# End of a fused attention and FFN kernel: PSUM banks, order of feature sums, and the engine of one elementwise pass

## The chip, the cores and the metric

The kernel runs on one core of one Trainium2 chip. The metric is device time in microseconds (us) for one execution, as the median of several. The engines are TensorE (PE, matmuls; its weight loads are shown as PEld), VectorE (DVE), ScalarE (ACT), GpSimd (POOL) and SyncE (SP, which issues the DMAs here). All engines run their own instruction streams and wait for each other by semaphores.

## The reference

Batch B = 8, H = 8 heads, S = 576 positions, head size 64. Attention with a threshold, then an FFN with ELU; everything is float32.

```python
scores = (1 / 8) * q @ k.transpose(0, 1, 3, 2)
thresh = max(scores, axis=-1) - tau
scores = where(scores >= thresh, scores, -1e9)
attn = softmax(scores)                      # sum + 1e-9 in the denominator
x = (attn @ v) arranged as (4608, 512)      # heads side by side
h = x @ w_in                                # w_in is 512 x 2048
g = where(h > 0, h, exp(min(h, 0)) - 1)
out = g @ w_out                             # w_out is 2048 x 512
```

## The kernel before

**Stages.** The program is one long sequence. In the first part the attention of the first sequences runs, with weights loaded beside it. At `banks.close()` (L661) the PSUM pools of that part end and pools named "ps_s2" (scores, 2 tiles of two banks), "ps_f2" (FFN results, 3 banks) and "ps_t2" (transposes and values, one bank) open: eight banks in all. From there on attention steps and FFN quarters are interleaved. When the attention has ended, at about 1172 us, only FFN is left. That last stretch is what most of the change is about.

**Groups of tokens.** The FFN goes by groups g of 512 tokens. Groups 0 to 7 are the first 512 positions of sequences 0 to 7 (group 0 is done early, in a plain form); group 8 is the last 64 positions of all eight sequences together (`xts[B]`, read back from `xtail`). A group's tokens fall in two halves of 256.

**Seven products instead of eight.** Both matrix products of a group are cut into 2 x 2 blocks and computed with seven block products (a Strassen-Winograd scheme), at the price of sums before and after.

- `first_product(g, u)` (u = 0 to 7), called a *unit* here and written (g, u): for two hidden tiles of 128 features and both token halves it issues seven products ("quarters", two 128x256 float32 matmuls, which the profile shows as four). Three PSUM banks (places 0, 1, 2) hold them. As results come: ACT copies place 0 (`w1`, L860), place 1 (`u2`) and place 2 (`s1`), POOL adds `w1` to `u2`, subtracts `u2` from `s1`, and after two more ACT copies (L913, L914) makes `t5` (L865); DVE adds `t5` and `s1` to PSUM (L868), one addition per half c = 0, 1 of the features. Product 3 writes on place 0 again, so it needs the `w1` copy done.
- ELU, in `exp(c)`, `minus` and `elu(c)`: ACT computes exp of the half (L879); then one is subtracted, for c = 0 by another ACT pass (L884), for c = 1 by a POOL pass (L893, `minus`); then DVE takes min and max with h (L902). This is the feature tile g.
- `sums` (L919 on): after each pair of units (v odd) four sums of feature tiles s1 to s4 (k = 0 to 3, shown as s, qm, e, vm, w, x by the buffer they lie in), for each c. The jobs go into the list `extra`. While attention runs (`attending[0]` true) POOL does them all (L938); afterwards POOL does k = 2 alone, DVE the others.
- `second_round(g, r)` (r = 0, 1): the product with w_out for the four hidden pairs of half r. For each of two chunks of 128 tokens (c) there are seven products of two quarters: k = 0 uses pairs v = 0, 1 and k = 1 uses v = 2, 3. Product 0 and 1 and 2 read g tiles, products 3 to 6 read feature sums. `ORDER` says which of three banks each product takes:

```python
ORDER = ((0, 0, 0), (0, 1, 1), (0, 2, 0), (0, 3, 2), (0, 4, 0), (1, 0, 1), (0, 5, 2), (0, 6, 0),
         (1, 3, 2), (1, 4, 0), (1, 2, 1), (1, 5, 2), (1, 1, 1), (1, 6, 0))   # (chunk, product, bank)
```

So products 0, 2, 4 and 6 of a chunk use one bank in turn. Product 2 adds onto product 0 after ACT has copied that (`snap`, L1004); product 4 begins anew in that bank once product 2 has been moved out by `final` (a DVE addition into `ot`, L1019, in round 1; an ACT copy, L1021, in round 0).

**Order.** The order on every engine is that in which the program records instructions, and it is written by a planner: `on_pe(cost, f)` advances a clock by 0.87 (`QT`) per quarter, `at(t, f)` puts a follow-up on an agenda for a planned time, and everything due is recorded before the next quarter. `ffn_quarters(n)` takes the next n quarters and puts each one's follow-ups (lists `after_`) on the agenda with their lags. Where a quarter needs features that are not recorded yet, the agenda is run on until they are (`ready`). `run_extra` and `need_extra` record jobs from `extra`.

**The end.** After the last attention step the rest of group 6 is run; all agenda work and `extra` are emptied (`until(1e9)`, `run_extra(99)`); then the pools are closed and one pool of six banks ("ps_f3") serves all that follows. `sums_x` (DVE, L737 to L739) makes sums of x for group 7 there. Then units and rounds run in the order (7,0) to (7,4), round (7, r=0), (7,5) to (7,7), (8,0), round (7, r=1), (8,1) to (8,4), round (8, r=0), (8,5) to (8,7), round (8, r=1). Jobs of `extra` are run after each quarter by `run_extra(0.9)`. Loads of weight sums (`sw`, `t`) and stores of `out` are issued by SP.

Of the kernel before, what the change touches and what calls it, by code (L numbers as in the profile page):

```python
# [10 lines left out]
FP32 = mybir.dt.float32  # L11
# [8 lines left out]
def kernel(  # L20
# [12 lines left out]
    P = 128  # L33
# [371 lines left out]
    CT = MAIN // 2  # L405
# [12 lines left out]
    def need_extra(*keys):  # L418
        mine = [x for x in extra if x[1] in keys]
        for x in mine:  # L420
            extra.remove(x)
            x[2]()
# [34 lines left out]
    def bank():  # L457
        return psum["f"].tile([P, 512], FP32, name="f", tag="f")
# [201 lines left out]
    assert units[0][1][0] == 1 and not pending  # L660
    banks.close()  # L661
    apart.append(True)
    for name, bufs in (("s", 2), ("f", 3), ("t", 1)):
        psum[name] = banks.enter_context(tc.tile_pool(name=f"ps_{name}2", bufs=bufs, space=PSUM))
    early.close()
    late["x"] = wpool[0] = ctx.enter_context(tc.tile_pool(name="late", bufs=1))

# [78 lines left out]
    with tc.manual_schedule():  # L746
# [50 lines left out]
        def at(t, f):  # L797
            serial[0] += 1
            heapq.heappush(agenda, (t, serial[0], f))
# [5 lines left out]
        def do_next():  # L805
            now[0], _, f = heapq.heappop(agenda)
            f()
# [17 lines left out]
        def first_product(g, u):  # L825
# [23 lines left out]
            def h(j, c):  # L849
                return gs[g, r, c][:, v, j].rearrange("p i t -> p (i t)")  # L850
# [16 lines left out]
            def add(o, x, name):  # L867
                nc.vector.tensor_tensor(o, place(x), loc[name], ALU.add)  # L868

            def exp(c):  # L870

                if attending[0] and (v < RU - 1 or c) and begun[0] + 0.3 < now[0] < begun[0] + 4.4:
                    at(begun[0] + 4.4, lambda: exp(c))
                    return
                e, last = ges.popleft()
                last()
                loc["e", c] = e
                ges.append((e, lambda: elu(c)))
                nc.scalar.activation(e, both(c), AF.Exp)  # L879
                if c:  # L880
                    loc["e1"] = e
                    at(now[0] + 1.6, minus)
                else:
                    nc.scalar.activation(e, e, AF.Copy, bias=-1.0)  # L884
                if attending[0] and (v < RU - 1 or c):
                    late_elus.append((now[0] + 1.2 * c, lambda: elu(c)))
                else:
                    at(now[0] + 1.4, lambda: elu(c))

            def minus():  # L890
                e = loc.pop("e1", None)
                if e is not None:
                    nc.gpsimd.tensor_scalar(e, e, 1.0, -1.0, ALU.mult, ALU.add)  # L893

            def elu(c):
                if ("elu", c) in loc:
                    return
                loc["elu", c] = True
                if c:
                    minus()  # L900

                nc.vector.scalar_tensor_tensor(both(c), loc["e", c], 0.0, both(c), ALU.min, ALU.max)  # L902
                ready.add((g, r, c, v))
                if v % 2:
                    sums(g, r, c, v - 1)
# [8 lines left out]
                [(0.1, lambda: nc.scalar.copy(h(1, 0), place(1))),  # L914
                 (0.55, lambda: pool("t5", lambda: h(1, 0), "u2", ALU.subtract))],
                [(0.6, lambda: add(h(0, 0), 2, "t5")), (1.3, lambda: exp(0))],
                [(0.1, lambda: add(h(1, 1), 0, "s1")), (1.4 if attending[0] else 0.7, lambda: exp(1))],
            )
            return [(lambda k=k: product(k), after_[k]) for k in range(7)]  # L919

# [5 lines left out]
        def sums(g, r, c, v):  # L926
            def one(k):
                gt = gs[g, r, c][:, v : v + 2]
                (a11, a21), (a12, a22) = ([gt[:, :, j, i] for i in range(2)] for j in range(2))
                if (r, c, k) in more:  # L930
                    cur[g, r, c, k] = more[r, c, k]
                if (g, r, c, k) not in cur:
                    cur[g, r, c, k] = late["x"].tile([P, RU, P], FP32, name=f"s{k}", bufs=1 if k else 2)
                s1, s2, s3, s4 = (cur.get((g, r, c, x)) for x in range(4))
                s1, s2, s3, s4 = (x if x is None else x[:, v : v + 2] for x in (s1, s2, s3, s4))
                o, x, y, op = ((s1, a21, a22, ALU.add), (s2, s1, a11, ALU.subtract),
                               (s3, a11, a21, ALU.subtract), (s4, a12, s2, ALU.subtract))[k]
                engine = nc.gpsimd if attending[0] or k == 2 else nc.vector  # L938
                engine.tensor_tensor(o, x, y, op)  # L939

            for k in range(4):
                job = (0.8, (g, r, c, k), lambda k=k: one(k))

                if c and k and (r, c, k) not in more and (g, r, k) not in ready:
                    waiting.setdefault((g, r, k), []).append(job)
                else:
                    extra.append(job)

        waiting, ready, attending = {}, set(), [True]
        ges = deque((late["x"].tile([P, 2 * CT], FP32, name="ge", bufs=2), lambda: None) for _ in range(2))  # L950
        late_elus = []

# [15 lines left out]
        def second_round(g, r):  # L968
            banks_ = []

            def chunk(c):
# [5 lines left out]
                def quarter(m, k):  # L977
# [11 lines left out]
                            do_next()  # L989
                    if left[0] == "s":  # L990
                        need_extra(*((g, r, c, x) for x in range(left[1] + 1)))
                    if right[0] == "t":
                        need_extra("out")
                    for v in range(2 * k, 2 * k + 2):
# [65 lines left out]
                    queue.append((first_product, (g, u)))  # L1060
                queue.append((second_round, (g, r)))

        quarters = deque()

        def ffn_quarters(n):
            while n and (quarters or queue):
                if not quarters:
                    f, a = queue.popleft()
                    quarters.extend(f(*a))
                p, posts = quarters.popleft()  # L1070
                end = on_pe(QT, p)
                for lag, f in posts:
                    at(end + lag, f)
                n -= 1
# [73 lines left out]
        for n in range(MIDDLE, len(steps) + 3):  # L1148
# [20 lines left out]
            ffn_quarters(before)  # L1169
            values_of(*steps[n - 3])  # L1170
            ffn_quarters(behind_)
        ffn_quarters(len(quarters))
        while queue:
            ffn_quarters(1)
            ffn_quarters(len(quarters))
        until(1e9)
        run_extra(99)

        attending[0] = False
        banks.close()
        psum["f"] = ctx.enter_context(tc.tile_pool(name="ps_f3", bufs=6, space=PSUM))
        ends[:] = [bank() for _ in range(6)]
        wide, narrow = wtp.tile([P, 3 * NT, NCH, T], FP32, name="wTb"), wtp.tile([P, 2 * NT, NCH, T], FP32, name="wTa")
        for c, t in enumerate((wide, narrow)):
            flat = t.rearrange("p g c n -> p (g c n)")[:, : RU * 4 * P]
# [8 lines left out]
            more[(1, *divmod(x, 4))] = t[:, : RU * P].rearrange("p (u t) -> p u t", t=P)  # L1196
        xts[B] = xpool.tile([P, KJ, MAIN], FP32, name="xt")
        nc.sync.dma_start(xts[B], xtail.rearrange("j p n -> p j n"))
        xs = [late["x"].tile([P, 2, CT], FP32, name=f"x{x}") for x in range(3)]
        for f in sums_x(B - 1, xs):  # L1200
            f()
        xs = [qkp.tile([P, S], FP32, name="qT") for _ in range(2)] + [qkp.tile([P, TAIL + S], FP32, name="kT")]
        xs = [x[:, : 2 * CT].rearrange("p (k t) -> p k t", k=2) for x in xs]
        late_sums = sums_x(B, xs)
# [5 lines left out]
        for x in order:  # L1210
            queue.append(x)
            if x == (first_product, (a, 6)):
                for f in late_sums:
                    f()
            ffn_quarters(1)
            while quarters:
                ffn_quarters(1)
                run_extra(0.9)
        until(1e9)


# [30 lines left out]
```

## Time and profile before

| What | Value |
|---|---|
| Median of 15 runs | 1389.43 us (1386.97 to 1394.93) |
| Profiled execution, its own time | 1387.78 us |
| Its span on the core | 1386.0 us |
| Mean TensorE clock granted, share of full speed | 0.993 |
| Last attention values on PE | 1172.7 us |
| Start of unit (7,0) | 1182.65 us |
| Start of unit (8,1) | 1287.07 us |
| Last result moved out of PSUM (DVE) | 1380.72 us |

Busy time of each engine in some windows of the last stretch, of 20 us each (the last 26 us):

| Window | PE | DVE | ACT | POOL |
|---|---|---|---|---|
| 1200 to 1220 | 19.70 | 12.24 | 9.17 | 8.92 |
| 1240 to 1260 | 19.52 | 13.68 | 10.61 | 11.38 |
| 1300 to 1320 | 19.69 | 11.62 | 9.18 | 7.81 |
| 1340 to 1360 | 18.31 | 13.36 | 9.31 | 10.37 |
| 1360 to 1386 | 20.69 | 7.48 | 0.37 | 5.33 |

How to read it: a profile is one execution. Busy time is that of instructions; matmuls overlap, so a PE that is busy all the time can still be slower than at its best, and the start times of matmuls tell more. A name such as "POOL s L939" is engine, tile written and line of the kernel. In brackets, and after an arrow, stands what ended an engine's idle time. After the last result there is a store and the end of the program, to 1386.0.

### The profile page before, as it was taken

How to read it: one execution, taken by the hardware profiler on the slowest of the kernel's cores; microseconds unless marked ns; L12 is line 12 of the kernel's file. 1: busy time of each engine (PE TensorE's matmuls, PEld its weight loads, DVE VectorE, ACT ScalarE, POOL GpSimd, SP SyncE). 2: the span in 40 equal slices, each digit the busy share in tenths (PEclk: the TensorE clock that was granted, in tenths of full speed). 3: DMA queues.
4: the chain of work that ended last, by engine and by line, in shares of the span. 5: the costliest groups of instructions: out<-in, count | busy, mean ns of one | idle time of the engine just before them, and what ended most of it. 6: DMA issues, size and time to landing. Idle time of an engine off the chain costs nothing.

```text
span 1386.0 us, 21954 instructions
## 1 busy us (share of the span) xinstructions
PE 1335.9 (96%) x6566; PEld 988.1 (71%) x6566; DVE 1066.8 (77%) x2362; ACT 632.9 (46%) x1387; POOL 829.4 (60%) x1331
## 2 busy tenths in 40 slices
PE   6897989999999999999999999999999999999998
PEld 4554745747777777777777777777777777888886
DVE  6777885988878887888788978888888874545533
ACT  5666665325454544445453636263636452422421
POOL 5567774878657564757475747675666646514422
PEclk9899999999999999999999999999999999999999
DMA  5245451588898989798888988898979785412211
GB/s 114 58 88 145 138 148 44 183 239 250 235 264 224 264 221 253 209 274 231 232 231 263 239 227 236 239 247 229 252 210 269 217 243 147 133 58 65 92 57 31
DMA packets 316342, 259.82 MB, mean 187 GB/s; under 512 B 208320, under 2 KB 272320, under 8 KB 316224
## 3 DMA queue, kind: packets, MB, share of 16 engines
q1 hardware_dynamic: 316224, 258.42, 67.7%
q8 instruction: 53, 0.87, 0.3%
q14 instruction: 65, 0.53, 0.1%
HBM read 167.84 MB, written 90.51 MB: 186 GB/s over the span
## 4 chain that ended last, share of the span: by engine, by line
PE 71%; DVE 10%; DMA 7%; ACT 5%; issue 3%; POOL 3%; SPq 2%; DVEq 0%; POOLq 0%; ACTq 0%
PE f L999 28%; PE f L846 18%; PE sc L238 10%; PE pv L388 8%; DMA there<-x 5%; PE f L475 3%; PE pv L384 2%; PE f L435 2%; DVE w L265 2%; DVE mx L1078 2%; ACT e L1088 2%; ACT e L253 1%; PE rt L277 1%; POOL wtop L143 1%; DVE x L348 1%
## 5 line engine op out<-in xcount | busy, mean ns | idle before, releaser
L274 POOL TENSOR_SCALAR w<-w,rs 128x576 f32<-128x576 f32 x288 | 246.8, 863 | 108.4 <-DVE rs L1104 75.0
L1078 DVE TENSOR_REDUCE mx<-sc 128x1 f32<-128x576 f32 x207 | 148.0, 752 | 82.9 <-PE sc L238 82.9
L238 PE MATMUL sc<-kT,qT 64*128 64x288 f32 x1024 | 182.7, 440 | 22.2 <-DVE w L265 11.5
L348 DVE STREAM_TRANSPOSE x<-w 128x512 f32<-128x512 f32 (+1 forms) x350 | 182.6, 568 | 8.3 <-POOL w L274 8.3
L1086 ACT ACTIVATE nb<-mx,nkeep 128x1 f32<-128x1 f32 x207 | 61.4, 297 | 253.2 <-DVE mx L1078 253.2
L1088 ACT ACTIVATE e<-sc,nb,keep 128x576 f32<-128x576 f32 x207 | 172.2, 832 | 6.9
L1097 DVE SCALAR_TENSOR_TENSOR w<-sc,th,e 128x576 f32<-128x576 f32 x207 | 163.1, 810 | 8.6 <-ACT e L1088 0.4
L238 PEld LDWEIGHTS sc<-kT,qT 64*128 64x128 f32 x1024 | 100.6, 190 | 87.1 <-issue 51.6
L846 PE MATMUL f<-xt,sw 128*128 128x256 f32 x512 | 129.0, 389 | 1.0 <-DVE ot L1017 0.5
L846 PE MATMUL f<-xt,w_in_sb 128*128 128x256 f32 x512 | 125.0, 383 | 1.7 <-ACT w L860 1.5
L1082 POOL TENSOR_SCALAR th<-mx,ntau 128x1 f32<-128x1 f32 x207 | 54.9, 266 | 111.6 <-DVE mx L1078 111.3
L846 PEld LDWEIGHTS f<-xt,sw 128*128 128x128 f32 x512 | 93.2, 190 | 29.9 <-issue 13.5
L846 PE MATMUL f<-x,w_in_sb 128*128 128x256 f32 x448 | 109.0, 382 | 5.5 <-ACT g L913 5.5
L253 ACT ACTIVATE e<-sc,nb,keep 128x576 f32<-128x576 f32 x81 | 65.2, 831 | 105.0 <-POOL nb L249 104.2
L846 PEld LDWEIGHTS f<-xt,w_in_sb 128*128 128x128 f32 x512 | 95.7, 190 | 22.1 <-ACT xs L400 4.6
L999 PE MATMUL f<-w_out_sb,s 128*128 128x256 f32 x448 | 109.4, 387 | 0.0
L999 PE MATMUL f<-t,s 128*128 128x256 f32 x448 | 106.7, 381 | 0.6 <-POOL s L939 0.6
L999 PE MATMUL f<-w_out_sb,g 128*128 128x256 f32 x448 | 107.2, 382 | 0.0
L846 PEld LDWEIGHTS f<-x,w_in_sb 128*128 128x128 f32 x448 | 84.1, 190 | 21.2 <-ACT g L913 10.3
L999 PEld LDWEIGHTS f<-w_out_sb,s 128*128 128x128 f32 x448 | 82.3, 190 | 23.0 <-issue 13.2
L999 PEld LDWEIGHTS f<-w_out_sb,g 128*128 128x128 f32 x448 | 84.0, 190 | 15.9 <-ACT ge L879 3.1
L999 PEld LDWEIGHTS f<-t,s 128*128 128x128 f32 x448 | 84.0, 190 | 14.3 <-POOL s L939 3.4
(162 smaller groups left out, 2546.9 us busy)
## 6 DMA issues: line engine op xcount, KB each, us to landing
there<-x SPq DMA_DIRECT2D x500, 144.0 KB, 4.2
wTb<-there SPq DMA_DIRECT2D x75, 576.0 KB, 4.6
wTa<-there SPq DMA_DIRECT2D x50, 576.0 KB, 4.3
sw<-win_sums SPq DMA_DIRECT2D x62, 384.0 KB, 4.6
t<-wout_sums SPq DMA_DIRECT2D x45, 512.0 KB, 5.3
qm<-in_q_dram SPq DMA_DIRECT2D x128, 72.0 KB, 4.0
vm<-in_v_dram SPq DMA_DIRECT2D x64, 128.0 KB, 4.3
wst<-in_moe_w_in_dram SPq DMA_DIRECT2D x16, 512.0 KB, 4.6
```

The lines of the kernel that those rows point to most:

```text
L238: nc.tensor.matmul(scs[h][:, a, :HALF], qs[r], kT[r, k0 : k0 + HALF], start=True, stop=True)
L253: nc.scalar.activation(e, st[h][:, :, :HALF], AF.Exp, bias=st["nb"][:, h : h + 1], scale=keep)
L274: nc.gpsimd.tensor_scalar(wv, wv, st["rs"][:, h : h + 1], 1.0, ALU.mult, ALU.mult)
L348: nc.vector.transpose(x[:, :, c0 : c0 + nc_], src.rearrange("p (c g n) -> p g c n", c=nc_, n=T))
L388: nc.tensor.matmul(pv[h * D : (h + 1) * D, g0 * T : g1 * T], vm[:, h, c], wT[:, g0:g1, h * (NC + 1) + c], start=False, stop=(c == NC - 1), ...
L846: nc.tensor.matmul(loc["banks"][place], left[:, j], right[:, j], start=(begins and j == 0), stop=(j == 1), skip_group_check=True)
L999: nc.tensor.matmul(place(m), lhs, rhs, start=(begins and v == 0), stop=(v == RU - 1), skip_group_check=True)
L1078: nc.vector.tensor_reduce(st["mx"][:, h : h + 1], st[h][:, :, :HALF], axis=AX.XY, op=ALU.max)
L1082: nc.gpsimd.tensor_scalar(st["th"][:, h : h + 1], st["mx"][:, h : h + 1], 1.0, ntau, ALU.mult, ALU.add)
L1086: nc.scalar.mul(st["nb"][:, h : h + 1], st["mx"][:, h : h + 1], nkeep)
L1088: nc.scalar.activation(e, st[h][:, :, :HALF], AF.Exp, bias=st["nb"][:, h : h + 1], scale=keep)
L1097: nc.vector.scalar_tensor_tensor(wv, sc[:, :, :HALF], st["th"][:, h : h + 1], e, ALU.is_ge, ALU.mult, accum_out=st["sm"][:, h : h + 1])
```

## The change

Four edits, all in the code around the end of the FFN:

1. **Banks.** At L663 the pool for f opens first and lives to the end of the kernel, so f has the first three banks, scores the next four, values the last. In the end stretch the pools of scores and values alone are closed, and their five banks join the three of f: eight banks in rotation instead of six new ones.
2. **Minus one.** Once attention has ended, the first half's subtraction (c = 0) is a POOL pass too, planned 0.7 after its exp; the exp of the second half is planned at lag 1.1 instead of 0.7.
3. **Sums.** `attending[0]` becomes false as soon as the attention loop has ended, ahead of the rest of group 6, so its last sums are spread over DVE and POOL. Sums of x for group 7 are put on the agenda there, 1.5 apart. Jobs of `extra` are no longer run by `run_extra(0.9)`: `quarter_and_sums` records one sum at a time at planned lags after certain quarters. Before a quarter uses a sum, the agenda is run until that sum of its pairs is recorded (`summed`).
4. **Last round.** The first seven quarters of round (8, r=1) are reordered: products 0, 1 and 3 first do their k = 0 quarter, then follow k = 1 of products 0 and 1, both quarters of product 2, and k = 1 of product 3.

Beyond that, the instructions up to the last attention steps are the same in the same order; SP's order is the same throughout. In the ordered lists of the two programs ACT has 16 instructions fewer (the L884 passes of the end stretch), and POOL and DVE differ in order and in which of them makes a sum. The diff, cut to its core:

```diff
-    for name, bufs in (("s", 2), ("f", 3), ("t", 1)):
-        psum[name] = banks.enter_context(tc.tile_pool(name=f"ps_{name}2", bufs=bufs, space=PSUM))
+    for name, bufs, stack in (("f", 3, ctx), ("s", 2, banks), ("t", 1, banks)):
+        psum[name] = stack.enter_context(tc.tile_pool(name=f"ps_{name}2", bufs=bufs, space=PSUM))
...
-                if c:
-                    loc["e1"] = e
-                    at(now[0] + 1.6, minus)
+                if c or not attending[0]:
+                    loc["minus", c] = e
+                    at(now[0] + (1.6 if c else 0.7), lambda: minus(c))
                 else:
                     nc.scalar.activation(e, e, AF.Copy, bias=-1.0)
...
-                if c:
-                    minus()
+                minus(c)
                 nc.vector.scalar_tensor_tensor(both(c), loc["e", c], 0.0, both(c), ALU.min, ALU.max)
...
-                [(0.1, lambda: add(h(1, 1), 0, "s1")), (1.4 if attending[0] else 0.7, lambda: exp(1))],
+                [(0.1, lambda: add(h(1, 1), 0, "s1")), (1.4 if attending[0] else 1.1, lambda: exp(1))],
...
                 engine.tensor_tensor(o, x, y, op)
+                summed.add((g, r, c, k, v))
...
                         need_extra(*((g, r, c, x) for x in range(left[1] + 1)))
+                        while not all((g, r, c, left[1], v) in summed for v in (0, 2)[: k + 1]):
+                            do_next()
...
                     f, a = queue.popleft()
-                    quarters.extend(f(*a))
+                    running[0] = f
+                    mine = f(*a)
+                    if (f, a) == (second_round, (B, 1)):
+                        mine = [mine[x] for x in (0, 2, 6, 1, 3, 4, 5)] + mine[7:]
+                    quarters.extend(mine)
...
-        ffn_quarters(len(quarters))
-        while queue:
+        attending[0] = False
+        xs = [late["x"].tile([P, 2, CT], FP32, name=f"x{x}") for x in range(3)]
+        for x, f in enumerate(sums_x(B - 1, xs)):
+            at(clock[0] + 2.0 + 1.5 * x, f)
+
+        def sum_on(pool):
+            for x in extra:
+                if (x[1][3] == 2) == pool:
+                    extra.remove(x)
+                    x[2]()
+                    return
+
+        def quarter_and_sums():
             ffn_quarters(1)
-            ffn_quarters(len(quarters))
+            k = 6 - len(quarters) if running[0] is first_product else None
+            for lag, pool in {None: ((0.3, False), (0.3, True)), 6: ((0.7, False),), 1: ((0.85, False),),
+                              3: ((0.8, False),), 4: ((0.75, True),)}.get(k, ()):
+                at(clock[0] + lag, lambda pool=pool: sum_on(pool))
+
+        while quarters or queue:
+            quarter_and_sums()
         until(1e9)
         run_extra(99)
-        attending[0] = False
         banks.close()
-        psum["f"] = ctx.enter_context(tc.tile_pool(name="ps_f3", bufs=6, space=PSUM))
-        ends[:] = [bank() for _ in range(6)]
+        psum["f"] = ctx.enter_context(tc.tile_pool(name="ps_f3", bufs=5, space=PSUM))
+        ends[:] = [bank() for _ in range(5)] + ends
...
-        xs = [late["x"].tile([P, 2, CT], FP32, name=f"x{x}") for x in range(3)]
-        for f in sums_x(B - 1, xs):
-            f()
...
-            ffn_quarters(1)
+            quarter_and_sums()
             while quarters:
-                ffn_quarters(1)
-                run_extra(0.9)
+                quarter_and_sums()
```

More of the change, by code (lines that the diff above doesn't have):

```diff
@@ L888, in exp, with minus @@
                     at(now[0] + 1.4, lambda: elu(c))
-            def minus():
-                e = loc.pop("e1", None)
+            def minus(c):
+                e = loc.pop(("minus", c), None)
                 if e is not None:
@@ L947, in sums @@
                     extra.append(job)
-        waiting, ready, attending = {}, set(), [True]
+        waiting, ready, summed, attending = {}, set(), set(), [True]
         ges = deque((late["x"].tile([P, 2 * CT], FP32, name="ge", bufs=2), lambda: None) for _ in range(2))
@@ L1061, in group @@
                 queue.append((second_round, (g, r)))
-        quarters = deque()
+        quarters, running = deque(), [None]
         def ffn_quarters(n):
```

## The prediction

> **What bounds the kernel now.** The page first. TensorE (PE) is busy 96% of the span; no other engine passes 77%.
>
> ```profile
> span 1386.0 us, 21954 instructions
> PE 1335.9 (96%) x6566; PEld 988.1 (71%) x6566; DVE 1066.8 (77%) x2362; ACT 632.9 (46%) x1387; POOL 829.4 (60%) x1331
> PE 71%; DVE 10%; DMA 7%; ACT 5%; issue 3%; POOL 3%; SPq 2%; DVEq 0%; POOLq 0%; ACTq 0%
> ```
>
> PE also carries 71% of the chain that ended last (third line). So a change counts by the PE idle time that it removes or makes. Next, PE's waits, kept to the stretch from 1150 us that the change rewrites:
>
> ```profile
> PE f L999 <- DVE wTb L902: 1.4, 1, 1.4
> PE f L846 <- ACT w L860: 1.3, 4, 0.3
> PE f L999 <- POOL s L939: 0.6, 2, 0.3
> PE f L846 <- DVE ot L1017: 0.5, 1, 0.5
> ```
>
> Idle time understates a stall, because the matmul after it starts up slower. So I price stalls from start times in PE's timeline. A quarter (four matmuls) advances 0.863 us; a product unit of seven quarters takes 6.04 (1188.80 to 1194.85 in one without a stall); a full product of the second round takes 1.73. Two pieces of that timeline, the fourth unit of group 7 and the end of group 8:
>
> ```profile
> 1200.89 1.89 PE L846 MATMUL f<-xt,sw 128*128 128x256 f32 x8
> 1202.62 1.03 PE L846 MATMUL f<-x,sw 128*128 128x256 f32 x4
> 1203.94 1.99 PE L846 MATMUL f<-xt,w_in_sb 128*128 128x256 f32 x8 [0.30 <-ACT w L860]
> 1207.50 1.89 PE L846 MATMUL f<-xt,sw 128*128 128x256 f32 x8
> ...
> 1348.08 1.89 PE L846 MATMUL f<-xt,sw 128*128 128x256 f32 x8
> 1351.15 1.99 PE L846 MATMUL f<-xt,w_in_sb 128*128 128x256 f32 x8 [0.32 <-ACT w L860]
> 1354.71 1.46 PE L999 MATMUL f<-w_out_sb,wTb 128*128 128x256 f32 x6
> 1357.54 0.70 PE L999 MATMUL f<-w_out_sb,wTb 128*128 128x256 f32 x2 [1.38 <-DVE wTb L902]
> 1358.08 1.89 PE L999 MATMUL f<-t,wTb 128*128 128x256 f32 x8
> ```
>
> Losses: unit (7,3) 6.61 - 6.04 = 0.57; likewise (7,7) 0.61, (8,0) 0.41, (8,3) 0.58, (8,7) 0.59. First product of the last round: 1358.08 - 1354.71 - 1.73 = 1.64. At the end of group 6: 0.53 at the sum s3 (1176.69, due 1176.26, then 0.10 slow) and 0.67 before group 7 (1182.65, due 1181.98).
>
> The L663 edit reaches further back: the pools renamed "2" open where the attention changes form. There PE stands too:
>
> ```profile
> 237.34 2.37 PE L388 MATMUL pv<-wTb,vm 128*64 128x320 f32 x16
> 240.03 0.42 ACT L400 COPY xs<-pv 64x64 f32<-64x64 f32 x2
> 240.51 1.24 PE L238 MATMUL sc<-kT,qT 64*128 64x288 f32 x8 [0.79 <-ACT xs L400]
> ```
>
> Sixteen pv matmuls take 2.30 elsewhere (1170.39 to 1172.69), so the scores were due at 239.64: 0.87 lost. All together 6.47 us.
>
> [...] the elu (L902) takes 0.69 us alone and 1.20 when POOL had just begun (1351.58 against 1351.51). [...]
>
> **Part 1, bank addresses.** With f allocated first, the first scores land on banks that DVE, not ACT's pv copies, released; its last pass there ended at 238.84, before 239.64. The first f tile now waits for the pv copies (end 240.23), but scores take 1.17, so it is due at 240.81: no wait. DVE, ACT and POOL idle 3.0, 2.6 and 4.6 us around there, and the later PE waits (262.87 on DVE, 0.92) follow from the scores, so all moves up. I take 0.87; bounds 0 (some later wait that does not move with the scores absorbs it) and 0.9.
>
> **Part 2, group 6 to 7.** The two s3 sums go to DVE and the s2 sums pass ahead of the t5 addition on POOL, so they are ready by about 1172: 0.53 gone. DVE now runs t5, x0, s3, x1 before the eviction at 1176.45: 1174.73 + 0.42 + 1.2 + 0.4 + 0.7, so it ends near 1177.6; the bank is needed at 1176.26 + 1.73 = 1177.98. Covered with 0.4 to spare; without cover it costs its lateness plus 0.1. Group 7 starts on banks free since 1173.3 instead of the 6-bank pool: 0.67 gone. SP's 1162 rows are the same in the same order, so no DMA moves past another. Sum 1.20; bounds 0.6 and 1.2.
>
> **Part 3, the minus-one pass.** ACT loses one 0.63 pass (0.54 of issue time) per unit, sixteen in all; POOL gains 16 x 0.62 = 9.9 us. ACT's order becomes exp first half, w1 copy of the next unit, exp second half, u2 copy. POOL's: minus first half, u2 addition, minus second half, s1, t5. The second minus therefore waits behind the u2 addition. Walk an odd unit, from its start 0: exp ends 6.88, minus 6.96 to 7.58, elu 7.62; exp second half 7.37 to 7.98; next u2 copy 7.97 to 8.34; u2 addition to 9.14; minus to 9.73; elu second half 9.77 to 10.97 (8.80 today). Then DVE: two sums of 0.97 and 0.76, so the next unit's addition (L868) starts at 12.63 (12.53 today, where a third sum stood before it). exp 13.14 to 13.77; w1 copy 13.66 to 14.01. It is due at 12.08 + 2.59 = 14.67, 0.66 to spare, where today it is late. In (8,0), c=1 sums add 1.85 on DVE: addition 18.98, exp 19.5, w1 ends 20.40, due 20.71. So 0.57 + 0.61 + 0.41 + 0.58 = 2.17 gone. If DVE is over 0.3 to 0.6 later, each stall returns in part: bounds 0.6 and 2.2. The rounds inside keep their cover: the snap copy of bank 0 (L1006) ends about 0.3 us early after (8,0), 1.1 early after (7,4).
>
> **Part 4, the last unit and reordered round.** (8,7) loses no time at w1 now: 0.59. The round starts with three quarters that need only old features, so the first late feature is due 2.59 + 0.43 = 3.02 after its start R, not 1.30. But DVE sums of c=1 come before the last addition, which starts at 18.98 after the start of (8,5), as today (1354.95 - 1335.99 = 18.96). exp, minus on POOL, elu: 20.86 to 21.55, so R + 3.43 with R = 18.12: about 0.5 lost. Next, the fifth product reuses bank 0 and waits for the eviction of the third (L1021). Today a whole product (1.73) lies between them; the third quarter moved forward leaves one quarter (0.86). DVE reaches L1021 after elu, sum, elu (behind POOL's s2 and minus), sum, sum, addition, sum, sum. Sums slowed by POOL as in today's rows give elu start + 5.8 to 6.0: 26.7 to 26.9, ends 27.2. Today the fifth product starts at 1363.26 - 1335.99 = 27.27. So the 0.59 + 1.64 = 2.23 saved are spent there: net 0. Bounds: DVE without slowing ends near 26, gain 1.2 to 1.6; slowed more, -0.7.
>
> **Sum.** 0.87 + 1.20 + 2.17 + 0 = 4.24. Against the profiled span, 1386.0 - 4.2 = 1381.8; that execution took 1387.78, so 1383.5. The median, 1389.43, lies 1.65 above it: 1385.2.
>
> **Rivals.** All of it: sums are not slowed because POOL's passes fall in gaps, so the last round also gains 1.2 to 2.2 and the time is about 1383.5. For: today's vm and w sums at 1349.19 took 0.41 each. Against: in the walk POOL's t5 and s2 stand exactly there.
>
> The stalls move: DVE is late enough that w1 stays late in four units and bank 0 costs 0.7 more, so parts 3 and 4 give nothing and only parts 1 and 2 hold, 1389.43 - 2.1 = 1387.3, no measurable change. For: slack of 0.3 in (8,0). Against: 0.66 in the others.
>
> GpSimd becomes the bound, slower. Its place is the sixteen product units. Rows today (busy, mean ns):
>
> ```profile
> L865 POOL TENSOR_TENSOR s<-s,u 128x256 f32<-128x256 f32 x16 | 15.5, 966 | 1.5 <-ACT s L860 0.6
> L865 POOL TENSOR_TENSOR u<-u,w 128x256 f32<-128x256 f32 x16 | 12.1, 759 | 31.8 <-ACT u L860 28.3 <-DVE x L738 3.5
> L893 POOL TENSOR_SCALAR ge<-ge 128x512 f32<-128x512 f32 x11 | 6.8, 620 | 27.6 <-ACT ge L879 27.6
> ```
>
> A unit holds 5.5 POOL operations on average afterwards, so it binds from 6.04 / 5.5 = 1.10 us each; today's mean is about 0.8. At 1.25, the longest row seen (1185.19), a unit takes 6.9: 16 x 0.84 = 13.4 lost against 4.2, 1398.6. It ends slower than before from 1.15 on. Against: the minus pass measures 0.62 throughout.
>
> **How the numbers follow.** Chances: the forecast 0.54 (own range 1384.2 to 1386.5), all of it 0.21, stalls move 0.17, GpSimd bound 0.08. A measurement of this kernel can tell about 0.2%, 2.8 us: under 1386.65 is faster. So faster 0.75, same 0.17, slower 0.08. The range reaches from the full gain, 6.47, 1383.0, a little wider for the median's own scatter, to the rival without change and 0.9 above: 1382.7 to 1388.2.
>
> **What would show it.** Right: no wait on xs at 240; no PE wait on w (L860) from 1180 us on; units of 6.04 throughout; in the last round a wait for bank 0 on DVE ot L1021 of about 1.7 with one on the elu (L901) of about 0.5. Wrong: PE waits on f from POOL or on w copies over 0.3, POOL rows of L893 over 0.9, or a last round without waits.

## The result, and the profile after

The changed kernel takes 1384.77 us (median of 9 runs, 1382.16 to 1386.12) beside 1389.62 us for the kernel before (45 runs, 1386.11 to 1394.93). The ratio is 0.9962, 95% interval 0.9953 to 0.9972: faster, by about twice the 0.2% that the prediction says can be told. A second session gave 0.9968 (0.9955 to 0.9980). The prediction was 1385.2.

The page of the changed kernel, as before the change: span, busy times, chain of waits by engine.

```profile
span 1383.3 us, 21964 instructions
PE 1337.4 (97%) x6566; PEld 991.6 (72%) x6566; DVE 1061.0 (77%) x2364; ACT 625.2 (45%) x1371; POOL 835.6 (60%) x1345
PE 75%; DVE 9%; ACT 5%; DMA 4%; issue 3%; POOL 2%; SPq 1%; DVEq 0%; POOLq 0%; ACTq 0%
```

PE's share of the chain rose from 71% to 75%. Its waits from 1150 us on (engine, line, what it waited for: us in total, times, longest):

```profile
PE f L1001 <- DVE ot L1021: 1.1, 1, 1.1
PE f L846 <- ACT g L912: 0.5, 1, 0.5
PE f L1001 <- POOL s L938: 0.3, 1, 0.3
```

The second and third lie before 1165 us, in attention. Of the waits shown before, on w1, on the elu, on s3 and before group 7, none is left; one is new, on L1021. PE's timeline around the switch at 240 us, around unit (7,3), and in the last round:

```profile
239.71 2.37 PE L388 MATMUL pv<-wTb,vm 128*64 128x320 f32 x16
242.01 1.24 PE L238 MATMUL sc<-kT,qT 64*128 64x288 f32 x8
...
1201.18 1.89 PE L846 MATMUL f<-xt,sw 128*128 128x256 f32 x8
...
1203.77 1.89 PE L846 MATMUL f<-xt,w_in_sb 128*128 128x256 f32 x8
...
1358.31 1.03 PE L1001 MATMUL f<-t,e 128*128 128x256 f32 x4
1360.43 1.99 PE L1001 MATMUL f<-w_out_sb,qm 128*128 128x256 f32 x8 [1.10 <-DVE ot L1021]
1362.26 1.89 PE L1001 MATMUL f<-w_out_sb,wTa 128*128 128x256 f32 x8
```

The scores follow the pv matmuls after 2.30 without a wait. Unit (7,3) runs through: 1201.18, then 2.59 later the fourth product. The last round stands once, at its fifth product: 1362.26 - 1358.31 - 2.59 = 1.36 lost.

To place the gain I compare the start of the same matmul (both programs issue 6566) in the two profiled executions, and take the differences between marks. This execution was already 2.36 us later at 217 us, and the change touches nothing before that. The loss falls between 18 and 27 us, where PE runs the same matmuls more slowly in it; the same eight score matmuls, in the kernel before and then in the changed one:

```profile
20.53 2.44 PE L238 MATMUL sc<-kT,qT 64*128 64x288 f32 x8
```

```profile
21.55 3.51 PE L238 MATMUL sc<-kT,qT 64*128 64x288 f32 x8
```

By 28 us both are equally fast (four score matmuls take 1.23 us in either): the first clock record of the trace, at the full clock, begins at 27.3 us in this execution and at 17.9 us in the other. From 217 us on:

| Stretch | predicted gain | measured |
|---|---|---|
| switch, 240 us | 0.87 | 0.86 |
| attention between | 0 | -0.12 |
| sum s3, end of group 6 | 0.53 | 0.54 |
| start of (7,0) | 0.67 | 0.79 |
| (7,3) | 0.57 | 0.57 |
| (7,7) and (8,0) | 1.02 | 1.01 |
| (8,3) | 0.58 | 0.58 |
| (8,7) and last round | 0 | 0.58 + 0.28 |
| all | 4.24 | 5.09 |

So 2.36 - 5.09 = -2.73, and the span is 1385.995 - 1383.268 = 2.73 shorter. The medians, 4.85 apart, agree with the 5.09.

The sum s3 and the start of (7,0) have no run of their own; the traces show how those stalls went. The two sums that PE waited for (k = 2; the prediction's part 2 calls them s2) were made by POOL behind one of its additions:

```profile
1175.23 0.72 POOL L1012 TENSOR_TENSOR t<-t,ot 128x256 f32<-128x256 f32 x1 [4.10 <-DVE t L1008]
1175.91 1.41 POOL L939 TENSOR_TENSOR s<-g 128x256 f32<-128x256 f32 x2
```

In the changed kernel they stand ahead of it, and DVE has taken over those of k = 3:

```profile
1172.83 1.41 POOL L938 TENSOR_TENSOR s<-g 128x256 f32<-128x256 f32 x2
```

Before the change, the first product of (7,0) waited for DVE's last eviction of group 6:

```profile
1182.18 0.42 DVE L1017 TENSOR_TENSOR ot<-f,u 128x256 f32<-128x256 f32 x1
```

Now it starts ahead of the same eviction, on a bank that was free:

```profile
1183.05 1.89 PE L846 MATMUL f<-xt,sw 128*128 128x256 f32 x8
1183.51 0.41 DVE L1019 TENSOR_TENSOR ot<-f,u 128x256 f32<-128x256 f32 x1
```

### The profile page after: what moved, and what is told of

Same layout as the page of the kernel before. It is cut to its first block, busy times and chain, and to the rows that moved or that the text cites. A ratio compares the mean times of both kernels' runs of the same rounds, so it can differ in the third digit from the quotient of the medians.

```text
span 1383.3 us, 21964 instructions
## 1 busy us (share of the span) xinstructions
PE 1337.4 (97%) x6566; PEld 991.6 (72%) x6566; DVE 1061.0 (77%) x2364; ACT 625.2 (45%) x1371; POOL 835.6 (60%) x1345
## 4 chain that ended last, share of the span: by engine, by line
PE 75%; DVE 9%; ACT 5%; DMA 4%; issue 3%; POOL 2%; SPq 1%; DVEq 0%; POOLq 0%; ACTq 0%
PE f L1001 27%; PE f L846 20%; PE sc L238 11%; PE pv L388 8%; PE f L475 3%; DMA there<-x 2%; PE pv L384 2%; PE f L435 2%; ACT e L1095 2%; DVE w L265 1%; DVE mx L1085 1%; PE rt L277 1%; ACT e L253 1%; POOL wtop L143 1%; DVE wtop L137 1%
## 5 line engine op out<-in xcount | busy, mean ns | idle before, releaser
L865 POOL TENSOR_TENSOR u<-u,w 128x256 f32<-128x256 f32 x64 | 49.1, 767 | 76.2 <-ACT u L860 76.2
```

## Experiments

Each run but the last two is a single execution. At 217 us, ahead of every edit, the profiled executions lie from 2.14 us before to 4.04 us after that of the kernel before, and waits in attention add up to 1.4, so single whole times are not compared. The marks inside one stretch of the FFN repeat to about 0.05 us, and the readings are made from them. Code is cut down to what differs; lines can begin in the middle.

**Pool order alone, on the kernel before.**

```diff
-    for name, bufs in (("s", 2), ("f", 3), ("t", 1)):
+    for name, bufs in (("f", 3), ("s", 2), ("t", 1)):
```

> The kernel before with only the order of the three PSUM pools at L663 changed (f, then s, then t); all else, the six new banks of the end too, stays. Theory: the stall on the xs copies at 240 us is a matter of addresses alone, so the PE timeline gains 0.87 us there and keeps it to the end of attention; the six new banks of the end take the places of the old f banks, so the start of unit (7,0) still loses 0.6 to 1.2 us, and the five stalls on w1 (0.57, 0.61, 0.41, 0.58, 0.59) and the 1.64 of the last round stay. Whole span 0.9 shorter. Rival: the wait on xs only changes its name or a later wait takes the gain, PE timeline unchanged (0.0 to 0.2) 20 us after it.

Measured: against the kernel before, the marks go from -1.65 us at 238 us to -2.52 at 250 and at 260: 0.87 gained. In PE's timeline the pv matmuls start at 235.69 and the scores follow at 238.00 without a wait.

The stall is one of addresses: whose old bank the scores fall on. At 385 us this execution stood 1.15 in a wait before values matmuls for which the profile shows no releaser. The same place shows 1.06 in the run with the sums alone below, which does not touch this part, 0.26 in the changed kernel and none in the kernel before; so it belongs, as far as these runs tell, to the execution and not to the edit. From 1165 us the marks stay within 0.05, with all stalls of before, the one ahead of (7,0) too.

**The minus-one pass alone, on the kernel before.**

```diff
-                if c:
-                    loc["e1"] = e
-                    at(now[0] + 1.6, minus)
+                if c or not attending[0]:
+                    loc["minus", c] = e
+                    at(now[0] + (1.6 if c else 0.7), lambda: minus(c))
```

> The kernel before with only the minus-one pass of the first half moved from ACT to POOL in the end stretch; exp lag, sums, banks and the last round stay. Theory: any one of three edits clears the w1 stalls, since w1 is late by only about 0.4 to 0.6 and this one takes 0.54 of issue time out of ACT's queue ahead of w1: each stall on w1 falls from 0.41-0.61 to at most 0.15, in sum 2.2 to 2.8 us less by the start of the last round. Rival: only the new places of the DVE sums clear them (the addition L868 that feeds exp is what is late), then here they stay within 0.2 of before each, sum under 1 us. Second rival: POOL in the way of its own passes: u2 and t5 are late and new PE waits on POOL appear, sum 0 or a loss.

**The lag alone, on the kernel before.**

```diff
-(1.4 if attending[0] else 0.7, lambda: exp(1))
+(1.4 if attending[0] else 1.1, lambda: exp(1))
```

> The kernel before with only the planned lag of the second half's exp at 1.1 instead of 0.7 after the last product, which puts it behind the next unit's w1 copy in ACT's queue. Theory: w1 starts about 0.5 us earlier, which is enough: stalls on w1 fall to at most 0.15 each, in sum 2.0 to 2.8 us less by the start of the last round; the last round itself then stands at the same waits as before or loses up to 0.5 more, since the second elu is later. Rival: the later exp delays elu and sums, and the next addition with them, so the stalls come back one unit later: sum under 1 us.

**The sums' places alone, on the kernel before.** `quarter_and_sums`, `sum_on` and `summed` as in the change, used in the loop over groups 7 and 8 only:

```diff
-            ffn_quarters(1)
+            quarter_and_sums()
             while quarters:
-                ffn_quarters(1)
-                run_extra(0.9)
+                quarter_and_sums()
```

> The kernel before with only the feature sums recorded one by one at the planned places in the units and rounds of groups 7 and 8 (group 6, banks, minus-one pass, exp lag and last round as before). Theory: DVE has one sum (0.76) less ahead of the addition L868 of the next unit, so exp and w1 come that much earlier, and the stalls in (7,3) and (8,3) go (0.57 and 0.58); (7,7), (8,0) and (8,7), where c = 1 sums are on DVE as well, go in part: sum 1.2 to 2.4 us by the start of the last round. Rival: w1 waits because ACT's own queue is full (two exp, one minus pass of 0.54 to 0.63 each), so earlier additions change nothing: sum under 0.5.

Measured for the three, as gains between the same marks (minus is a loss); the rounds between the units are 0 where not named:

| Stretch | changed kernel | minus alone | lag alone | sums alone |
|---|---|---|---|---|
| (7,3) | 0.57 | 0.57 | -0.37 | 0.55 |
| (7,7) and (8,0) | 1.01 | 0.86 | -0.88 | 0.97 |
| (8,3) | 0.58 | 0.57 | -0.35 | 0.57 |
| (8,7) | 0.58 | 0.59 | -0.28 | 0.58 |
| three rounds before the last | 0 | 0 | -3.66 | 0 |
| last round | 0.28 | -2.54 | -1.04 | 0.40 |
| all | 3.02 | 0.05 | -6.58 | 3.07 |

By the start of the last round the minus alone has gained 2.59 (2.2 to 2.8 expected) and the sums alone 2.67 (1.2 to 2.4 expected).

Three things follow. First, the minus pass and the sums each clear the w1 stalls without the other, so their gains do not add. Around the end of unit (7,3), DVE and ACT in the kernel before, where w1 ends at 1203.89 and PE needs it at 1203.48:

```profile
1197.59 1.20 DVE L902 SCALAR_TENSOR_TENSOR g<-ge,g 128x512 f32<-128x512 f32 x1 [0.54 <-POOL ge L893]
1200.56 0.83 DVE L939 TENSOR_TENSOR s<-g,s 128x256 f32<-128x256 f32 x1
1201.32 0.41 DVE L868 TENSOR_TENSOR g<-f,t 128x256 f32<-128x256 f32 x1
1202.48 0.63 ACT L884 ACTIVATE ge<-ge 128x512 f32<-128x512 f32 x1
1203.54 0.35 ACT L860 COPY w<-f 128x256 f32<-128x256 f32 x1
```

ACT with the minus alone, and then DVE and ACT with the sums alone:

```profile
1202.69 0.62 ACT L879 ACTIVATE km<-g 128x512 f32<-128x512 f32 x1
1203.21 0.35 ACT L860 COPY w<-f 128x256 f32<-128x256 f32 x1
```

```profile
1200.92 0.42 DVE L868 TENSOR_TENSOR g<-f,t 128x256 f32<-128x256 f32 x1 [0.62 <-POOL t L865]
...
1202.10 0.63 ACT L884 ACTIVATE ge<-ge 128x512 f32<-128x512 f32 x1
...
1203.15 0.35 ACT L860 COPY w<-f 128x256 f32<-128x256 f32 x1
```

With the minus alone, the pass between the two exps (L884) is gone and w1 ends at 1203.56, where PE needs it at 1203.98. With the sums alone, all three passes still stand before w1, but the addition L868 waits for no sum any more, only for t5, and w1 ends at 1203.50, needed at 1203.65. That is a margin of 0.15 us: enough here, and no more.

Second, the minus pass alone gains nothing in all, since it loses 2.54 in the last round. PE stands 2.23 us for the elu, which takes 1.08 us beside a POOL pass where it took 0.69, and then PE runs at half speed (its granted clock is 0.50):

```profile
1356.30 0.70 PE L998 MATMUL f<-w_out_sb,wTb 128*128 128x256 f32 x2 [2.23 <-DVE wTb L901]
1356.84 2.76 PE L998 MATMUL f<-t,wTb 128*128 128x256 f32 x8
```

The products that start at 1356.84 and 1359.39 (the next row) advance 2.55 and 2.59 where 1.73 is usual: 1.68 lost on top of the wait. So 0.86 of the 2.54 comes from the later elu and 1.68 from the clock, which did not fall after a longer pause in another run (see the end); without that fall, by these figures, the minus pass alone would have gained about 1.7.

Third, the lag alone is a loss, and the theory for it was wrong in number and in idea. POOL and DVE of that run, whose unit (7,3) starts 2.87 us later than in the kernel before:

```profile
1200.41 0.72 POOL L865 TENSOR_TENSOR u<-u,w 128x256 f32<-128x256 f32 x1 [2.97 <-ACT u L860]
1201.10 0.61 POOL L893 TENSOR_SCALAR ge<-ge 128x512 f32<-128x512 f32 x1
...
1201.75 1.21 DVE L902 SCALAR_TENSOR_TENSOR g<-ge,g 128x512 f32<-128x512 f32 x1 [1.75 <-ACT g L913]
...
1205.06 0.42 DVE L868 TENSOR_TENSOR g<-f,t 128x256 f32<-128x256 f32 x1
```

The exp behind w1 (1199.43, after w1 at 1199.18) pushes its minus pass behind POOL's u2 addition, the second elu starts 1.29 later than before (1201.75 against 1197.59 + 2.87), three sums follow it, and the next addition is 0.87 late (1205.06 against 1201.32 + 2.87): more than the 0.5 that w1 won in ACT's queue. The rival named in its expectation was right in mechanism; the stalls came back larger, and the snap copies at the rounds (ACT s L1004, 0.93 three times) came late as well. The pass and the lag together without the sums, the form that the prediction's part 3 had in mind, were not run.

**The changed kernel without the reordering of the last round.**

```diff
-                    if (f, a) == (second_round, (B, 1)):
-                        mine = [mine[x] for x in (0, 2, 6, 1, 3, 4, 5)] + mine[7:]
```

> The changed kernel with only the reordering of the last round's first seven quarters taken out. The kernel before with only the sums placed anew ran as fast in the end stretch as the changed kernel, so this asks what the reordering is for. Theory: with the first half's minus-one pass on GpSimd the last elu is late (it ends at about 2.7 us after the start of the last round, where the second quarter pair needs it at 0.86), so without the reordering PE stands 1.4 to 1.7 us at the elu of (8,7) and no wait for bank 0 is left: loss of the round 1.6 to 1.9 where the changed kernel loses 1.36, so the end comes 0.2 to 0.6 us later. Rival, by the run with the minus pass alone: GpSimd's sum stands ahead of the minus pass and the elu is 0.9 us later than that: loss 2.5, end 1.1 to 1.3 us later. Third: the reordering does nothing, difference under 0.15.

**The changed kernel with the minus-one pass back on ACT** (lag back at 0.7).

```diff
-                if c or not attending[0]:
+                if c:
                     loc["minus", c] = e
...
-(1.4 if attending[0] else 1.1, lambda: exp(1))
+(1.4 if attending[0] else 0.7, lambda: exp(1))
```

> The changed kernel with the minus-one pass of the first half back on ACT and the exp lag back at 0.7; banks, sums and reordering as changed. Theory: the sums' new places alone clear the w1 stalls, so the units stay at 6.04 us (no wait on w over 0.1), and the second elu of (8,7) starts about 0.4 us earlier, so the wait for bank 0 on DVE ot (L1021) falls from 1.10 to 0.6-0.8: the end comes 0.3 to 0.5 us earlier than in the changed kernel. Rival, the prediction's own account of part 3, in which the pass taken off ACT is what pays for 0.54 of each stall: w1 stalls of 0.2 to 0.6 come back in (7,7), (8,0) and (8,7), where DVE carries c = 1 sums: 0.6 to 1.5 us later.

Measured for these two, from 1184 us to the end: without the reordering 0.17 us later (0.2 to 0.6 expected), with the minus pass on ACT 0.31 us earlier (0.3 to 0.5 expected), and no wait on w comes back. PE's only wait from 1165 us on is, without the reordering, 1.27 for the elu (DVE wTb L901), and with the minus pass on ACT 0.78 for bank 0 (DVE ot L1021).

With the run on the sums alone, these give all four combinations of order and minus pass, each with its lag. Loss in the last round, worked out from start times as in the prediction; the kernel before loses 1.64:

| Sums at their new places, and | order as before | reordered |
|---|---|---|
| minus on ACT | 1.24 | 1.05 |
| minus on POOL | 1.54 | 1.36 |

So the reordering is worth 0.2, the minus pass on POOL costs 0.3, and the sums are worth 0.4 here. In the end stretch after group 6, the sums alone give what all edits together give (3.07 against 3.02), and without its edit of the minus pass the changed kernel came out 0.31 faster there.

**More work for GpSimd.** The changed kernel, with two idle passes per unit.

```diff
+            def load():
+                if idle:
+                    nc.gpsimd.tensor_scalar(idle[0], idle[0], 1.0, 0.0, ALU.mult, ALU.add)
...
-(0.55, lambda: pool("u2", nm("u2"), "w1", ALU.add))]
+(0.55, lambda: pool("u2", nm("u2"), "w1", ALU.add)), (0.56, load)]
...
-(0.55, lambda: pool("t5", lambda: h(1, 0), "u2", ALU.subtract))]
+(0.55, lambda: pool("t5", lambda: h(1, 0), "u2", ALU.subtract)), (0.56, load)]
```

> The changed kernel with two more GpSimd passes (128x512, about 0.62 us each) in each of the sixteen product units of groups 7 and 8, one behind the u2 addition and one behind t5, on a tile that nothing else uses; results unchanged. GpSimd then has about 4.3 + 1.25 = 5.5 us of work per unit of 6.04. Theory (GpSimd far from being the bound): the units keep 6.04 to 6.3 us; s1 comes 0.6 later but the addition that needs it is over a product away; the first half's additions wait for t5 no longer than before; the whole costs 0 to 2 us. Rival (GpSimd becomes the bound as its passes are held up by VectorE to 1.0 us and more): units grow to 6.6 to 7.0, 9 to 15 us in all.

Measured, from 1184 us to the end: 6.16 us lost, between the two ranges expected. Busy times of each engine in three windows of 20 us each (from 1200, 1240 and 1300 us), their sum and mean; the last figure, the mean of POOL, is the one to read:

```profile
sum 60.00, PE 58.60 PEld 49.47 DVE 40.13 ACT 22.02 POOL 47.30; mean PE 19.53 PEld 16.49 DVE 13.38 ACT 7.34 POOL 15.77
```

In the changed kernel the same windows have a mean of 11.23 us on POOL, and 35.03 in sum on DVE. POOL is now at 79%, from 56%, and not full; DVE's time grows by 15% beside it. The losses are not spread evenly over the units, as the rival had them, but sit mostly at waits: PE on the snap copy (0.44 three times), once on w1 (0.79), on the elu of (8,7) (1.53) and on bank 0 (1.27). So neither account was right: the load costs time well before GpSimd is full. Part of that is the order of its queue, as passes that others wait for stand behind the idle ones (ahead of the first snap copy an idle pass starts at 1211.90, the minus pass follows at 1212.48, and DVE has stood 1.79 for it); part is that the passes lengthen each other (t5 from a mean of 0.85 to 0.90 us to 1.06). How much each does was not separated.

**Bank 0.** The changed kernel, with the eviction L1021 of the third product of the last round's first chunk taken off DVE:

```diff
+                    elif r and (g, c) == (B, 0):
+                        z = late["x"].tile([P, 3, 2, P], FP32, name="sw", bufs=2)[:, 0].rearrange("p k f -> p (k f)")
+                        nc.scalar.copy(z, place(m))
+                        nc.gpsimd.tensor_tensor(o, z, o, ALU.add)
                     elif r:
                         nc.vector.tensor_tensor(o, place(m), o, ALU.add)
```

> The changed kernel, with the eviction of the third product of the last round's first chunk (L1021) moved from VectorE: ACT copies the bank to a free tile and GpSimd adds it to ot. Theory: the fifth product waits for nothing but this eviction behind VectorE's queue of sums, so the 1.10 wait goes, and with it 1.1 to 1.4 us of the end. Rival: the sums and elu that stand in VectorE's queue are needed by the next products anyway, so the wait moves to them (a wait on a vm, w or e sum at L1001 of 0.5 to 1.0): 0 to 0.6 us.

Measured: 1.37 us earlier at the end (1.1 to 1.4 expected). ACT copies the bank as soon as the product is done, and the fifth product starts on time, 0.86 after the quarter ahead of it (1357.59):

```profile
1357.79 0.37 ACT L1022 COPY sw<-f 128x256 f32<-128x256 f32 x1 [2.16 <-PE f L1001]
...
1358.45 1.89 PE L1001 MATMUL f<-w_out_sb,qm 128*128 128x256 f32 x8
```

From 1165 us to the end PE waits for nothing. The wait was for DVE's queue and not for the data.

**A version better than both.** With that, what is left is mostly in attention, outside the change: eleven times, 72.7 us apart, PE stands 0.50 us for the copy L912, which waits in ACT's queue behind the pass nb of the step with one head, and nb waits for the row maximum. The second edit plans nb and exp of that step 0.3 later:

```diff
-                at(t + 2.1 + 1.05 * h, lambda h=h: exp_of(pr, i, h))
+                at(t + (2.1 if len(hs) > 1 else 2.4) + 1.05 * h, lambda h=h: exp_of(pr, i, h))
```

> The changed kernel once more, beside the next one on the same chip: 0.9962 of the kernel before, within 0.9950 to 0.9975.

> The changed kernel with two further edits. One is that of the run on bank 0 (1.37 us measured there). The other: in an attention step of one head the exp (with the small pass nb ahead of it) is planned 0.3 us later, behind the copy L912 of the FFN unit, which today waits in ACT's queue behind nb, which waits for the row maximum; PE stands 0.50 us eleven times for that copy. Theory: each of the eleven costs 0.66 us of start time and 0.10 of slow start, so eleven times 0.76 = 8.4 us go, with bank 0 9.7 us: ratio to the changed kernel 0.993, to the kernel before 0.989. Rival: the exp, later by a copy, holds up the softmax chain of its step (mask, transposes, values), and PE's wait moves there: 0 to 3 us of the 8.4 remain.

Measured: the changed kernel again 1384.87 us, ratio to the kernel before 0.9968 (0.9955 to 0.9980); with both edits 1378.37 us, 0.9918 (0.9902 to 0.9934), 6.5 us less than the changed kernel. Expected were 9.7, so the edit in attention gave about 5.1 and not 8.4. ACT around the first of the eleven places, in the changed kernel and then with the edit:

```profile
422.02 0.29 ACT L1093 ACTIVATE nb<-mx,nkeep 128x1 f32<-128x1 f32 x1 [1.98 <-DVE mx L1085]
...
423.08 0.36 ACT L912 COPY g<-f 128x256 f32<-128x256 f32 x1
```

```profile
421.72 0.37 ACT L912 COPY g<-f 128x256 f32<-128x256 f32 x1 [1.27 <-PE f L846]
422.44 0.29 ACT L1097 ACTIVATE nb<-mx,nkeep 128x1 f32<-128x1 f32 x1 [0.34 <-DVE mx L1089]
```

All eleven waits are gone and bank 0 gave its 1.37 again. Exp is not held up by the copy: nb waits for the maximum (DVE mx) in both. In PE's waits from 390 to 1165 us others stand instead, this one and two smaller, 0.53 for the elu of the last step (DVE g L901) and 0.2 for another transfer (wTb):

```profile
PE pv L384 <- DMA wTa<-there: 1.3, 2, 0.9
```

The elu comes just behind where the eleventh stall was and had been covered by it. The DMA waits, about 2.3 us in start times, stand between 460 and 500 us. A like wait (0.22) showed at 459 us in the run with the minus pass alone, which changes nothing there, so DMA waits come without the edit too; whether this edit makes them likelier was not settled.

## Why the prediction was right, and where it was not

**Bounds and prices.** That PE's idle time alone counts held: the marks add up to the whole difference. Pricing a stall by start times and not by its gap held too: removing gaps of 0.30 moved the end by 0.57. Of the 0.27 between, 0.10 is the slower restart (1.99 us beside 1.89 for eight matmuls), and 0.17 lies in the row ahead of the gap, which lasts 1.03 where a quarter advances 0.86.

**Part 1, bank addresses.** 0.87 predicted, 0.86 and, alone, 0.87 measured. In the changed kernel nothing later took it back. The pv copies end at 240.46 and not at 240.23, which is the first of two; both lie before 240.81, so nothing hung on it.

**Part 2, group 6 to 7.** 0.54 and 0.79, 1.33 where 1.20 was said and 1.2 was the upper bound. The term for the start of (7,0) was mis-sized: 0.67 left out the slow restart behind that stall, 0.10, which the prediction had counted at s3.

**Part 3, the minus-one pass.** The sum was right (2.17; 2.16 measured), and so was the walk's first half: second elu at 1198.92 where the walk gives 1189.09 + 9.77 = 1198.86. The next addition came at 1201.25 and not at 1201.72, since the first of the two sums took 0.41 and not 0.97; so w1 had 1.10 to spare and not 0.66. What failed is the account. The step put the gain down to ACT's order, 0.54 off by the minus pass and exp behind w1, and treated the third sum as a detail. The runs show two sufficient causes, the minus pass alone 2.00 and the sums alone 2.09, and that exp behind w1, taken alone, costs 6.58 by the end. Either account gives the same sum, so the right 2.17 does not speak for the one given: there it was luck.

**Part 4, the last unit and reordered round.** 0.59 at (8,7) was right (0.58), and so was the form of one loss, a wait for bank 0 on L1021. "Net 0" was not: 0.86 was kept. The failing step is the price of DVE's sums, "slowed by POOL as in today's rows". DVE of the changed kernel, from the sums of c = 1 before the last addition to the eviction:

```profile
1351.63 0.83 DVE L938 TENSOR_TENSOR w<-vm,wTa 128x256 f32<-128x256 f32 x1
1352.39 0.41 DVE L868 TENSOR_TENSOR wTb<-f,t 128x256 f32<-128x256 f32 x1
...
1354.26 0.69 DVE L901 SCALAR_TENSOR_TENSOR wTb<-ge,wTb 128x512 f32<-128x512 f32 x1 [0.80 <-POOL ge L893]
...
1359.97 0.41 DVE L1021 TENSOR_TENSOR ot<-f,ot 128x256 f32<-128x256 f32 x1
```

(8,5) starts at 1334.13, so the addition is at 18.26 (18.98 predicted), the elu at 20.13 (20.86) and L1021 ends at 26.25 (27.2). Most of that lead comes ahead of the addition: the two sums there, 0.41 and 0.83, begin at 1351.19 and hold it to 1352.39, 1.20 where the walk has 1.85. Of the eight sums up to L1021, five take 0.41 or 0.42 and three 0.83. No wait on the elu was left, where about 0.5 was said, and bank 0 cost 1.36 and not 1.7. Before the second elu (1356.62) DVE stands 1.20 for POOL's minus pass, queued behind a sum; the walk had that.

**Rivals.** "All of it" was right that POOL's passes would slow fewer sums, but where it has 1.2 to 2.2 for the last round, 0.28 was gained. "The stalls move" did not happen. "GpSimd becomes the bound" was rightly held unlikely, since the minus pass keeps 0.62 to 0.67; but a price by capacity alone (from 1.10 us for each operation) comes out too low, as the added load showed: with GpSimd at 79%, 6.2 us were gone.

**The number.** The errors are 0.13 in part 2, 0.86 in part 4, and 0.12 the other way in attention: 4.24 becomes 5.09, but for 0.02 of rounding. That the median still stands only 0.4 below the prediction is in part luck: the medians moved by 4.85 and not by 5.09, and that of the kernel before went from 1389.43 to 1389.62 with more runs.

## What to carry over

When several edits aim at one stall, each may be enough alone: find the margin by which the waited-for pass is late (0.41 us in unit (7,3)) and compare every edit with it before adding gains, and try an edit without its companions, because one (here the later exp) may be a cost that another covers. A queue worked off in order can cost time before its engine is full (6.16 us with GpSimd at 79%): ask what stands between a short pass that others wait for and the head of its queue, and move the one that waits, as with L1021 and with nb. A copy by an idle engine that frees a PSUM bank can be worth more than the pass it adds: here 1.37 us for 0.37 on ACT and 0.91 on POOL.

## What the runs showed of the hardware

**After a pause PE's clock may fall to half, and after a like pause it may not.** In the run with the minus pass alone, PE stood 2.23 us, and 1.4 us after it had restarted its clock fell to half. One window of that run (its bounds, its length, PE busy, granted clock, DMA share, GB/s); the two after it are alike:

```profile
1358.00:1359.00 1.00, 1.00 (x4) 0.50 0.00 0
```

The half clock lasted 3.4 us and cost 1.68. In the run with the lag alone, PE stood 2.42 us at the same place, and the clock stayed at 1.00. Attention shows the same at about 200 us, where PE stands some 1.9 us for DVE in each of the twelve profiled executions. In nine the clock then fell to half for 3.4 us, in three it stayed at 1.00. Here is the kernel before, with the fall, and then the second session's execution of the changed kernel, without it:

```profile
201.39 1.49 PE L238 MATMUL sc<-kT,qT 64*128 64x288 f32 x8 [1.93 <-DVE w L265]
...
204.39 2.98 PE L388 MATMUL pv<-wTb,vm 128*64 128x320 f32 x16
```

```profile
203.77 1.24 PE L238 MATMUL sc<-kT,qT 64*128 64x288 f32 x8 [1.90 <-DVE w L265]
...
205.79 2.37 PE L388 MATMUL pv<-wTb,vm 128*64 128x320 f32 x16
```

Two pauses of about 1.73 us, near 138 and 184 us, were followed by no fall in any of the twelve. In the kernel before, the clock stood at 0.50 also for 10.2 us from 62.3 us on; PE had just stood 0.75 us there, and no wait of the 14 us before was longer. What decides whether the clock falls was not shown.

**VectorE beside GpSimd: who starts first.** The same sum of 128x256 takes 0.41 us on DVE or 0.82 to 0.95, by whether a POOL pass is under way when it begins. Around the eviction in the changed kernel:

```profile
1357.23 0.42 DVE L938 TENSOR_TENSOR e<-qm,wTb 128x256 f32<-128x256 f32 x1
1357.39 0.84 POOL L938 TENSOR_TENSOR w<-wTa 128x256 f32<-128x256 f32 x1 [0.81 <-DVE wTa L901]
1357.68 0.83 DVE L938 TENSOR_TENSOR vm<-wTb,e 128x256 f32<-128x256 f32 x1
```

Counted over both kernels from 1165 us on, the 57 sums on DVE that began with no POOL pass under way took 0.41 to 0.43, even where one began during them; of the 41 that began during one, 39 took 0.82 to 0.95, the other two 0.49 and 0.74. It works the other way too: POOL's subtraction s (L865) went from a mean of 0.97 us to 0.74, and 12 of its 16 passes began during a sum or elu of DVE before the change, none after it. So where a pass falls changes both prices (0.41 or 0.83 for a sum, 0.97 or 0.74 for s), and the prediction's walk lost most of its accuracy there, in parts 3 and 4.
